# Reordered first loads, small vector steps moved to GpSimd and paired last folds in a spectral filter and token MLP kernel

## The chip, the cores and the metric

The kernel runs on one core of a Trainium2 chip. The metric is the device time of one execution in microseconds: the median of three runs is 124.67 us (124.54 to 124.88). All times below are microseconds unless a row says ns.

## The reference

Two branches work on the same x of 2048 tokens by 512 channels (bf16), and a sigmoid gate mixes them:

```python
def _A_ref(x, w_r, w_i):                       # spectral filter
    X = rfft2(x.astype(float32), axes=(-2, -1))
    X = X * (w_r + 1j * w_i)
    return irfft2(X, s=(S, D)).astype(bfloat16)

def _B_ref(x, w1, b1, w2, b2):                 # MLP over tokens
    h = _layernorm(x, axis=-1)
    u = gelu(einsum("bsd,sf->bdf", h, w1) + b1)
    y = einsum("bdf,fs->bds", u, w2) + b2
    return y.transpose(0, 2, 1)

g = sigmoid((x * gate_w).sum(-1, keepdims=True))
out = g * a + (1 - g) * b                      # a, b: the two branches; S=2048, D=512, F=1792
```

## The kernel before

The 2048 tokens lie on 128 partitions in 16 blocks of 512 channels. Block j = 4q + r holds the tokens of quarter q whose number leaves r when divided by 4.

**The MLP branch** fills most of TensorE. m1 (L710) multiplies w1 by the normalized x (h) into 14 hidden tiles; a gelu on ScalarE (L730) writes them to gl. m2 (L1103) multiplies w2 by gl into one PSUM bank y per output block, 14 matmuls each. ScalarE evicts y with the gate and the bias (yev, L1121), for the last two blocks VectorE does (fin, L1151).

**The spectral branch** takes four stages, each a set of small matmuls on TensorE, an eviction on ScalarE and sums and differences on VectorE:
- forward along the tokens: folds of x over q (q4a L550, q4s L555, q4b L560), matmuls fa (L572 to L575), copies (L578), butterflies (L584, radix4 L603 to L619);
- forward along the channels: matmuls fb (L669), copies (L673), folds eo into B (L683 to L688);
- the filter: butterfly bfly (L810), products with W (L818), comb (L823), ob (L847 to L849) back into B. Some bins need a path of their own. c0a (L786) copies the first bins of B to c0; c0b (L831 to L841) multiplies them with the filter's ends into ce; c0c (L853) puts ce back into B. nyq (L801 to L804) multiplies a single line on one partition into nn. ScalarE's queue then moves that line and eight lines of B into s9 by two DMAs ("lines"), one matmul (linem, L866) and a copy to s8 follow, and a DMA puts it back into B;
- inverse along the tokens: radix4 again, matmuls i1, i1h and i1o (L899, L913, L952 to L955), copies, folds zh, zg and zf (L926 to L971), the closing fold fq (L977, L978) once for each half h;
- inverse along the channels: matmuls i3 (L1036, L1037), evictions with the gate (L1040, L1089, L1091), a GpSimd copy "ends" (L1108), the folds L1111 to L1116, and the sum with y (L1139).

The gate: x times gate_w on VectorE (L738), row sums on ScalarE (L743), a tanh (L746), and omg (L750 to L753), four small operations that make 1 - g and the scaled bias.

**The order of the work.** Each step is added to a plan with an engine, a duration, its reads and writes and a priority. The plan runs a list schedule with these durations, in which each engine takes the ready step of the lowest priority, and the program is written out in the order that results. So each engine's queue is fixed before the run, and a queue whose next instruction waits holds back all that stands behind it.

**GpSimd's queue before.** It issues some loads, then 16 gathers of rows of the filter (L771) paced by one-element copies that wait for h or gl (L760), then the loads of the tables tg and ti, and at the end the copies L1108.

**The first loads before.** SP issues x block 0, then w1 blocks 0, 2 and 1, the table ta and w1 block 3; ScalarE issues x blocks 2, 1 and 3 before its first table load. Of the four blocks with r = 0, VectorE makes the layernorm statistics of blocks 0 and 4, ScalarE those of 8 and 12 (ASTAT).

Of the kernel before, what the change touches and what calls it, by code (L numbers as in the profile page):

```python
# [16 lines left out]
P = 128  # L17
S = 2048
D = 512
# [115 lines left out]
class Plan:  # L135
# [32 lines left out]
    def order(self):  # L168
# [17 lines left out]
        while events:  # L186
# [16 lines left out]
            while progress:  # L203
                progress = False
                for eng, ts in pending.items():
# [15 lines left out]
                    if best.pk:  # L221
                        n, size = best.pk[:2]
                        k = best.pk[2] if len(best.pk) > 2 else 16
                        work = n * (0.009 + size / 27200.0)
                        issue = max(now, lanes[-8] if len(lanes) > 7 and eng != "POOL" else 0.0) + best.dur
                        dma_free = max(dma_free, issue + 0.8) + work / 16 * (1.45 if issue < 2.0 else 1.2 if issue < 6.0 else 1.0)
# [44 lines left out]
def kernel(  # L271
# [14 lines left out]
    V, A, T = nc.vector, nc.scalar, nc.tensor  # L286
# [78 lines left out]
    add("ACT", 0.4, presq, reads=["eps"], writes=["omg"], prio=-8.85)  # L365
# [107 lines left out]
    ASTAT = (8, 12, 5, 2)  # L473
# [3 lines left out]
    for r in range(4):  # L477
# [10 lines left out]
        for n, j in enumerate(OWN[r]):  # L488
# [11 lines left out]
            else:  # L500
                add("DVE", 0.82, lambda j=j: stat(j), reads=[("x", r, j // 4)], writes=[("mv", j)], prio=pj, after=[n0] if j == 4 else ())
# [4 lines left out]
            if j == 0:  # L506
                s0 = sj
            if j == 8:
                aq.deps.add(s0)
# [9 lines left out]
            if j == 8:  # L519
                n8 = nj  # L520
# [26 lines left out]
        def q4a(r=r):  # L547
            xf = t["xf", r] = t["gl"][:, 6 + 4 * (r % 2):10 + 4 * (r % 2), :]
            xs = t["x"][:, :, r, :]
            V.tensor_sub(xf[:, 2:4], xs[:, 0:2], xs[:, 2:4])  # L550

        def q4s(r=r):
            xs = t["x"][:, :, r, :]
            s = t["st"][:, 0:1024].rearrange("p (m d) -> p m d", m=2)
            V.tensor_add(s, xs[:, 0:2], xs[:, 2:4])  # L555
# [7 lines left out]
        add("DVE", tt(1024), q4s, reads=xk, writes=["st"], prio=pq, after=[n8])  # L563
        add("DVE", tt(1024), q4a, reads=xk, writes=[("xf", r % 2)], prio=pq, alloc=["xf"])
        add("DVE", 2 * tt(512), q4b, reads=["st"], writes=[("xf", r % 2)], prio=pq)
# [157 lines left out]
    for n, (ft, j, cs) in enumerate(order):  # L723
        last = j == jorder[-1]
        bank = "fb" if 4 <= ft < NF else "acc"
        m1t.append(add("PE", mm(cs.stop - cs.start), lambda ft=ft, j=j, cs=cs: m1(ft, j, cs),
# [22 lines left out]
    def omg():  # L749
        V.tensor_scalar(t["omg"][:], t["g"][:], -0.5, 0.5, op0=Alu.mult, op1=Alu.add)  # L750
        V.tensor_scalar(t["g"][:], t["g"][:], 0.5, 0.5, op0=Alu.mult, op1=Alu.add)
        V.tensor_scalar_mul(t["g"][64:P, 1::2], t["g"][64:P, 1::2], 0.5 ** 0.5)
        V.tensor_mul(t["ombb2"][:], t["omg"][:], t["b2f"][:])  # L753
    add("DVE", 0.5, omg, reads=["b2f"], writes=["g", "omg"], prio=0)
# [29 lines left out]
    def c0a():  # L784
        b = t["B"][:, :, :, :, 0]
        V.tensor_copy(t["c0"][:, 0], b[:, :, :, 0:2])  # L786
        V.tensor_copy(t["c0"][:, 1], b[:, :, :, 3:1:-1])
    add("DVE", 0.2, c0a, reads=[("B", lt, e) for lt in range(2) for e in range(4)], writes=["c0"], prio=0.3)

    for lt in range(2):  # L790
# [3 lines left out]
        if lt == 0:  # L794
            def nyq():
# [4 lines left out]
                for i in range(2):  # L800
                    V.tensor_mul(na[:, i], v, wn[:, i, None, 0:L].to_broadcast([1, 2, L]))  # L801
                V.tensor_sub(nn[:, 0], na[:, 0, 1], na[:, 1, 0])
                V.tensor_add(nn[:, 1], na[:, 1, 1], na[:, 0, 0])
                V.tensor_mul(nn[:, ::-1, 0], t["c0"][0:1, 1, 0, 0, :], wn[:, 0, 0:257:256])  # L804
            add("DVE", 2 * tt(512) + 2 * tt(256) + 0.1, nyq, reads=bk + [("wn", 0), ("wn", 1), "c0"] + pbk, writes=["nn"], prio=0.5)
# [20 lines left out]
        if lt == 0:  # L826
            def wprep():
# [3 lines left out]
                V.tensor_add(pv[0], ends[0][:, :, 0], ends[0][:, :, 1])  # L831
                V.tensor_sub(pv[1], ends[1][:, :, 0], ends[1][:, :, 1])

            def c0b():
                wprep()
                c0, cm, ce, pm = t["c0"], t["cm"], t["ce"], t["wpm"]
                for i in range(2):
                    V.tensor_mul(cm[:, i], c0[:, i, None].rearrange("p o a e k -> p o (a e) k").to_broadcast([P, 2, 8, 2]),
                                 (pm[:] if i == 0 else pm[:, ::-1]).rearrange("p i a e k -> p i (a e) k"))
                V.tensor_sub(ce[:, 0], cm[:, 0, 0], cm[:, 1, 0])  # L840
                V.tensor_add(ce[:, 1], cm[:, 0, 1], cm[:, 1, 1])  # L841
            add("DVE", tiny(4) + 0.25, c0b, after=[cb], reads=["c0"] + [("W", c, l) for c in range(2) for l in range(2)], writes=["ce"], prio=0.3)
# [73 lines left out]
    for h in range(2):  # L916
# [13 lines left out]
        def zg(h=h):  # L930
            e, o = t["zp"][:, h, 0], t["zp"][:, h, 1]
            z = t["zz"][:, h, 1].rearrange("p v k r a -> p r (v k) a")[:, 1::2]
            V.tensor_add(z[:, :, :, 0:64], e, o)
            V.tensor_sub(e, e, o)
            V.tensor_sub(z[:, :, 0::2, 64:P], e[:, :, 0::2], e[:, :, 1::2])
            V.tensor_add(z[:, :, 1::2, 64:P], e[:, :, 0::2], e[:, :, 1::2])
        add("DVE", 2 * tt(512) + 2 * tt(256), zg, reads=[("zp", h, 0), ("zp", h, 1)], writes=[("zz", h, 1, 1), ("zz", h, 3, 1)], prio=3.55)

        for r in (0, 2):
# [21 lines left out]
            def zf(h=h, r=r):  # L961
                e = t["ze"][:, h, r // 2]
                k0, k1 = (t["zz"][:, h, :, :, k, r, :] for k in range(2))
                if r == 0:
                    V.tensor_copy(k0[:, :, :, 0], e[:, :, :, 0])
                    V.tensor_copy(k1[:, :, :, 0], e[:, :, :, P])
# [5 lines left out]
            add("DVE", 2 * tt(512) + (tiny(2) if r == 0 else 0), zf, reads=[("ze", h, r, lt) for lt in range(2)], writes=[("zz", h, r, lt) for lt in range(2)], prio=3.55)  # L972
# [6 lines left out]
        add("DVE", 2 * tt(2048), fq, reads=[("zz", h, r, lt) for r in range(4) for lt in range(2)] + [("T", 0, 0), ("T", 0, 1), ("T", 1, 0), ("T", 1, 1)], writes=["xs" if h == 0 else "pp", ("z", h)], prio=3.54 if h == 0 else 3.6)  # L979
# [93 lines left out]
    for grp in groups:  # L1073
        for j in grp:
# [35 lines left out]
            def fold(e, o, s):  # L1110
                V.tensor_add(s[:, 0, :, 1:P], e[:, :, 1:P], e[:, :, P + 1:L])  # L1111
                V.tensor_sub(s[:, 1, :, P - 1:0:-1], e[:, :, 1:P], e[:, :, P + 1:L])
                sv = s.rearrange("p k (j h) d -> p j h k d", h=2)
                for u in range(o.shape[1]) if o.shape[1] == 1 else (slice(None),):
                    V.tensor_add(o[:, u, 0:4:3], sv[:, u, 0], sv[:, u, 1])
                    V.tensor_sub(o[:, u, 2:0:-1], sv[:, u, 0], sv[:, u, 1])  # L1116
            quart = lambda v: v.rearrange("p j h (k d) -> p j (h k) d", k=2)

            if j < LATE:
# [4 lines left out]
                if j % 2 == 0:  # L1124
                    continue

                def pair(j=j):
                    return (epair(j // 2 % NEO) if j > 1 else t["e0"]).rearrange("p j h d -> p (j h) d")
                ek = [("eo", 0, 0), ("eo", 0, 1)] if j == 1 else [("eo", j - 1), ("eo", j)]
                add("POOL", 0.4, lambda j=j, ends=ends, pair=pair: ends(pair(), espair(j // 2)), reads=ek, writes=[("es", j // 2 % 2)], prio=4)  # L1130

                def es(j=j, fold=fold, quart=quart, pair=pair):
                    fold(pair(), quart(epair(NEO + j // 2 % NOB)), espair(j // 2))
                add("DVE", 4 * tt(512), es, reads=ek + [("es", j // 2 % 2)], writes=[("ob", j)], prio=4, alloc=["ob"], free=["eo"] if j > 1 else ())

                def fin(j=j):
                    tbuf(j)
                    o = t["tb_"][:, j - 1:j + 1]
                    V.tensor_add(o, o, epair(NEO + j // 2 % NOB))  # L1139
                add("DVE", tt(1024), fin, reads=[("ob", j)], writes=[("o", j - 1), ("o", j)], prio=4, free=["ob"])  # L1140
            else:
                add("POOL", 0.4, lambda j=j, ends=ends: ends(epair(j // 2 % NEO)[:, j % 2], espair(j)[:, :, 0:2]), reads=[("eo", j)], writes=[("es", j % 2)], prio=4)

                def es(j=j, fold=fold, quart=quart):
                    fold(epair(j // 2 % NEO)[:, j % 2], quart(tbuf(j)[:, None]), espair(j)[:, :, 0:2])
                add("DVE", 4 * tt(256), es, reads=[("eo", j), ("es", j % 2)], writes=[("o", j)], prio=4, free=["eo"] if j % 2 else (), after=gates)

                for n, cs in enumerate(parts):
                    def fin(j=j, n=n, cs=cs):
                        o = tbuf(j).rearrange("p h d -> p (h d)")[:, cs]  # L1150
                        V.scalar_tensor_tensor(o, t["y", j, n][:, cs], t["omg"][:, j:j + 1], o, op0=Alu.mult, op1=Alu.add)  # L1151
                    add("DVE", d1(cs.stop - cs.start) + 0.1, fin, reads=[("y", j, n), "omg", ("o", j)], writes=[("of", j, n)], prio=1,
                        free=[("acc", "fa")[n]])

# [41 lines left out]
```

## Time and profile before

| | before |
|---|---|
| median of three runs | 124.67 us |
| profiled execution, its own time | 124.94 us |
| its span in the trace | 123.2 us |
| TensorE's first m1 matmul, end of the last m2 | 5.06, 120.34 us |
| TensorE, VectorE, ScalarE, GpSimd busy | 118.0, 113.8, 84.9, 42.2 us |
| granted TensorE clock | 1.0 |

Times in the rows count from the start of the span. A row of the timeline gives the start, the busy time, the engine (DVE is VectorE, ACT ScalarE, POOL GpSimd, SP the sync engine's DMA queue), the line, the operation and its tiles and shapes. In brackets stands how long the engine was idle before, and what ended that. A row of the chain in order of time gives the start, the length and the step.

### The profile page before, as it was taken

To read this page: it belongs to the slowest core of one execution; us is meant where nothing else is said; L and a number is where in the kernel's file an instruction comes from. 1 tells how busy PE (TensorE), PEld (TensorE's weight loads), DVE (VectorE), ACT (ScalarE), POOL (GpSimd) and SP (SyncE) were. 2 spreads that over 40 slices of the span, in tenths; PEclk is the share of its full clock that TensorE was granted. 3 is DMA by queue.
4 is the path that set the end of the run, shared out by engine and by line. 5 is a ranking of instruction groups with operands and counts; after the bars stand their busy time and mean duration, and the time that the engine had idled before them with its cause. 6 is when DMAs were issued, how large, how long until landed. Compare 5 with 4: busy or idle time off the path is not lost.

```text
span 123.2 us, 2197 instructions
## 1 busy us (share of the span) xinstructions
PE 118.0 (96%) x760; PEld 65.6 (53%) x774; DVE 113.8 (92%) x248; ACT 84.9 (69%) x182; POOL 42.2 (34%) x57
## 2 busy tenths in 40 slices
PE   6998999999999999999999999999999999999990
PEld 2454555546544666444455545557565566655570
DVE  1799999999999979999999999999999999999991
ACT  3869999997998699988420047238993369979500
POOL 6502428988089984889100000000000002112300
PEclk9999999999999999999999999999999999999999
DMA  3999999999999999999728800000000000214062
GB/s 95 286 366 365 366 374 195 245 351 324 340 289 197 169 284 385 397 406 343 222 39 318 340 0 3 0 0 5 3 0 5 1 0 3 118 55 176 0 255 85
DMA packets 16765, 22.80 MB, mean 185 GB/s; under 512 B 3216, under 2 KB 13858, under 8 KB 16754
## 3 DMA queue, kind: packets, MB, share of 16 engines
q1 hardware_dynamic: 15122, 19.71, 51.7%
q0 software_dynamic: 1152, 2.55, 7.5%
q10 hardware_dynamic: 480, 0.40, 1.0%
q8 instruction: 6, 0.10, 0.4%
q14 instruction: 5, 0.04, 0.1%
HBM read 20.54 MB, written 2.10 MB: 184 GB/s over the span
## 4 chain that ended last, share of the span: by engine, by line
PE 87%; DMA 7%; ACT 2%; issue 1%; DVE 0%; SPq 0%
PE acc L1103 39%; PE acc L710 30%; DMA x<-in_A_x_dram 7%; PE fb L710 4%; PE fb L669 1%; PE fa L669 1%; PE fa L574 1%; PE fa L575 1%; PE fa L572 1%; PE fa L1036 1%; PE fa L913 1%; PE fb L1037 1%; PE fa L1037 1%; PE fb L1036 1%; PE fa L899 1%
## 5 line engine op out<-in xcount | busy, mean ns | idle before, releaser
L1103 PE MATMUL acc<-gl,wb 128*128 128x512 bf16 (+1 forms) x124 | 31.3, 376 | 0.3 <-issue 0.2
L710 PE MATMUL acc<-h,wb 128*128 128x512 bf16 x124 | 29.7, 379 | 0.2
L1103 PE MATMUL acc<-gl,wa 128*128 128x512 bf16 (+1 forms) x93 | 23.5, 376 | 0.2
L1103 PEld LDWEIGHTS <-wb 128*128 128x128 bf16 x136 | 14.4, 113 | 10.6 <-issue 0.2
L710 PEld LDWEIGHTS <-wb 128*128 128x128 bf16 x128 | 12.2, 98 | 12.4
L1121 ACT ACTIVATE x<-acc,ombb,omg 128x512 bf16<-128x512 f32 x14 | 11.0, 784 | 10.0 <-PE acc L1103 7.6
L710 PE MATMUL acc<-h,wa 128*128 128x512 bf16 (+1 forms) x67 | 16.9, 371 | 0.0
L1108 POOL COPY st<-zo 128x8 bf16<-128x8 bf16 x1 | 0.4, 442 | 42.9 <-DVE zo L1061 42.9
L1103 PEld LDWEIGHTS <-wa 128*128 128x128 bf16 x102 | 10.8, 113 | 7.8
L710 PEld LDWEIGHTS <-wa 128*128 128x128 bf16 x102 | 10.0, 99 | 9.2 <-DMA wa<-in_B_w_dram 0.9
L771 POOL DMA_INDIRECT W<-in_A_w_i_dram,ix x8 | 14.1, 1766 | 1.8 <-issue 1.8
L730 ACT ACTIVATE gl<-acc,b1f 128x512 bf16<-128x512 f32 x12 | 8.3, 693 | 4.6 <-PE acc L710 4.5
L482 DVE BATCH_NORM_STATS2 stats<-x 128x6 f32<-128x512 bf16 x12 | 8.2, 680 | 2.2 <-DMA x<-in_A_x_dram 2.2
L743 ACT ACTIVATE x<-x 128x512 bf16<-128x512 bf16 x16 | 9.9, 623 | 0.0
L771 POOL DMA_INDIRECT W<-in_A_w_r_dram,ix x8 | 9.3, 1166 | 1.6 <-issue 1.3
L710 PE MATMUL fb<-h,wa 128*128 128x512 bf16 (+1 forms) x32 | 9.6, 366 | 0.1
L578 ACT CAST xp<-fa 128x512 bf16<-128x512 f32 x16 | 8.9, 578 | 1.0 <-issue 0.6
L1108 POOL COPY st<-X 128x8 bf16<-128x8 bf16 (+1 forms) x8 | 3.2, 412 | 11.7 <-ACT X L1040 8.8
L543 ACT ACTIVATE h<-x,nmr,rstd 128x512 bf16<-128x512 bf16 x8 | 6.3, 803 | 0.0
L868 ACT CAST s<-fa 8x512 bf16<-8x512 f32 x1 | 0.6, 575 | 8.2 <-PE fa L866 8.2
L669 PEld LDWEIGHTS <-X 128*128 128x128 bf16 x64 | 4.7, 98 | 2.4 <-issue 0.2
L760 POOL COPY hold<-gl 1x1 bf16<-1x1 bf16 x6 | 4.2, 695 | 4.8 <-ACT gl L730 4.8
(190 smaller groups left out, 254.2 us busy)
## 6 DMA issues: line engine op xcount, KB each, us to landing
wb<-in_B_w_dram SPq DMA_DIRECT2D x8, 512.0 KB
wb<-in_B_w_dram SPq DMA_DIRECT2D x2, 2048.0 KB
wa<-in_B_w_dram SPq DMA_DIRECT2D x1, 3072.0 KB
wa<-in_B_w_dram SPq DMA_DIRECT2D x2, 768.0 KB
out_dram<-x SPq DMA_DIRECT2D x3, 512.0 KB
x<-in_A_x_dram SPq DMA_DIRECT2D x2, 512.0 KB
wa<-in_B_w_dram SPq DMA_DIRECT2D x4, 192.0 KB
wa<-in_B_w_dram SPq DMA_DIRECT2D x2, 384.0 KB
```

What stands on the lines that cost most here:

```text
L482: V.bn_stats(out=t["stats"][:, j, :], in_=t["x"][:, j // 4, j % 4, :])
L543: add("ACT", act(512, 2), lambda j=j: A.activation(t["h"][:, j // 4, j % 4, :], t["x"][:, j // 4, j % 4, :], ActF.Identity, bias=t["nmr"][ ...
L578: add("ACT", act(512), lambda r=r, dq=dq: A.copy(xa(r)[:, :, :, dq, :], t["pa", r, dq][:]), reads=[("pa", r, dq)], writes=[("X", r % 2, dq ...
L669: T.matmul(pb[:, q, :, b, :], lhsT=t["X"][:, lt, e, c, 2 * b + q, :], rhs=t["tb"][:, k:k + 128], start=True, stop=True)
L710: T.matmul(t["u", ft][:, cs], lhsT=w[:, j // 4, j % 4, c * P:(c + 1) * P], rhs=t["h"][:, j // 4, j % 4, cs], start=(j == jorder[0] and not ...
L730: gelus.append(add("ACT", act(512, 1), lambda ft=ft: A.activation(t["gl"][:, ft, :], t["u", ft][:], ActF.Gelu_apprx_tanh, bias=t["b1f"][:, ...
L743: A.activation(t["x"][:, q, r, :], t["x"][:, q, r, :], ActF.Copy, accum_out=t["glog"][:, 4 * q + r:4 * q + r + 1])
L760: nc.gpsimd.tensor_copy(t["hold"][:], t["h"][0:1, n // 4, n % 4, 511:512] if kind == "h" else t["gl"][0:1, n, 0:1])
L771: add("POOL", 1.15, lambda comp=comp, lt=lt, e=e: nc.gpsimd.indirect_dma_start(out=t["W"][:, comp, lt, e, 1, 0:257], out_offset=None, in_= ...
L1103: T.matmul(t["y", j, n][:, cs], lhsT=w[:, o, 512 * q + r:512 * q + 512:4], rhs=t["gl"][:, ft, cs], start=(ft == 0), stop=(ft == NFT - 1))
L1108: nc.gpsimd.tensor_copy(s[:, :, :, 0], e[:, :, 0:129:128].rearrange("p m k -> p k m"))
L1121: A.activation(tbuf(j).rearrange("p h d -> p (h d)"), t["y", j, 0][:], ActF.Identity, bias=t["ombb2"][:, j:j + 1], scale=t["omg"][:, j:j + 1])
```

## The change

It has three parts. The line numbers of the steps in the changed kernel are higher by 2 to 20.

First, SP issues x block 0, x block 2, w1 block 0, x block 1, and w1 blocks 2, 1 and 3; ScalarE loads its table first and then issues x block 3 and ta. Statistics of block 8 go to VectorE and those of block 4 to ScalarE. The folds q4a and q4s of r = 0 are split in two halves, the first of them before the first h. Some durations and priorities of the plan change with it.

Second, omg, c0a, nyq, c0b and the two small copies of zf (now zc) are issued on GpSimd instead of VectorE.

Third, the fold of the last stage is split into two steps, folda and foldb, and blocks 14 and 15 are folded as one pair, as the others are, with their y added after. zg is split into zga and zgb, with its difference written to st instead of in place.

```diff
-    ld_x0(2, "ACT", -9)
+    ld_x0(2, "SP", -8.95)
     ld_w10(0, "SP", -8.9)
-    ld_x0(1, "ACT", -8.9)
-    ld_x0(3, "ACT", -8.88)
+    ld_x0(1, "SP", -8.85)
+    ld_x0(3, "ACT", -8.9)
...
-    ld_ta(0, -8.65)
+    ld_ta(0, -8.8, "ACT")
...
-    add("ACT", 0.4, presq, reads=["eps"], writes=["omg"], prio=-8.85)
+    add("ACT", 1.6, presq, reads=["eps"], writes=["omg"], prio=-8.95)
...
-    ASTAT = (8, 12, 5, 2)
+    ASTAT = (4, 12, 5)
...
+        if r == 0:
+            for m in range(2):
+                xm = [("x", 0, m), ("x", 0, m + 2)]
+                add("DVE", tt(512), lambda q4a=q4a, m=m: q4a(m=slice(m, m + 1)), reads=xm, writes=[("xf", 0, m)], prio=pq,
+                    alloc=[] if m else ["xf"], after=[n8] if m else ())
+                add("DVE", tt(512), lambda q4s=q4s, m=m: q4s(m=slice(m, m + 1)), reads=xm, writes=[("st", m)], prio=pq,
+                    after=[n8] if m else [b8])
...
     def omg():
-        V.tensor_scalar(t["omg"][:], t["g"][:], -0.5, 0.5, op0=Alu.mult, op1=Alu.add)
+        G.tensor_scalar(t["omg"][:], t["g"][:], -0.5, 0.5, op0=Alu.mult, op1=Alu.add)
...
-    add("DVE", 0.5, omg, reads=["b2f"], writes=["g", "omg"], prio=0)
+    add("POOL", 1.2, omg, reads=["b2f"], writes=["g", "omg"], prio=0)
...
-        V.tensor_copy(t["c0"][:, 0], b[:, :, :, 0:2])
-        V.tensor_copy(t["c0"][:, 1], b[:, :, :, 3:1:-1])
-    add("DVE", 0.2, c0a, reads=[("B", lt, e) for lt in range(2) for e in range(4)], writes=["c0"], prio=0.3)
+        G.tensor_copy(t["c0"][:, 0], b[:, :, :, 0:2])
+        G.tensor_copy(t["c0"][:, 1], b[:, :, :, 3:1:-1])
+    add("POOL", 0.7, c0a, reads=[("B", lt, e) for lt in range(2) for e in range(4)], writes=["c0"], prio=0.3)
...
                 for i in range(2):
-                    V.tensor_mul(na[:, i], v, wn[:, i, None, 0:L].to_broadcast([1, 2, L]))
+                    G.tensor_mul(na[:, i], v, wn[:, i, None, 0:L].to_broadcast([1, 2, L]))
...
-            add("DVE", 2 * tt(512) + 2 * tt(256) + 0.1, nyq, reads=bk + [("wn", 0), ("wn", 1), "c0"] + pbk, writes=["nn"], prio=0.5)
+            add("POOL", 3.2, nyq, reads=bk + [("wn", 0), ("wn", 1), "c0"] + pbk, writes=["nn"], prio=0.5)
...
-                V.tensor_add(pv[0], ends[0][:, :, 0], ends[0][:, :, 1])
-                V.tensor_sub(pv[1], ends[1][:, :, 0], ends[1][:, :, 1])
+                G.tensor_add(pv[0], ends[0][:, :, 0], ends[0][:, :, 1])
+                G.tensor_sub(pv[1], ends[1][:, :, 0], ends[1][:, :, 1])
...
-            add("DVE", tiny(4) + 0.25, c0b, after=[cb], reads=["c0"] + [("W", c, l) for c in range(2) for l in range(2)], writes=["ce"], prio=0.3)
+            add("POOL", 2.0, c0b, reads=["c0"] + [("W", c, l) for c in range(2) for l in range(2)], writes=["ce"], prio=0.3)
...
+            if r == 0:
+                def zc(h=h):
+                    e = t["ze"][:, h, 0]
+                    G.tensor_copy(t["zz"][:, h, :, :, 0, 0, 0], e[:, :, :, 0])
+                    G.tensor_copy(t["zz"][:, h, :, :, 1, 0, 0], e[:, :, :, P])
+                add("POOL", 0.7, zc, reads=[("ze", h, 0, lt) for lt in range(2)], writes=[("zc", h)], prio=3.5)
...
+            if j % 2:
+                k = j // 2
...
+                add("DVE", 2 * tt(512), lambda k=k, pair=pair, folda=folda: folda(pair(), espair(k)), reads=ek, writes=[("ef", k % 2)], prio=4,
+                    free=["eo"] if j > 1 else ())
+                add("DVE", 2 * tt(512), lambda k=k, obuf=obuf, foldb=foldb: foldb(obuf(), espair(k)), reads=[("es", k % 2), ("ef", k % 2)],
+                    writes=ok, prio=4, alloc=["ob"] if j < LATE else (), after=gates)
```

More of the change, by code (lines that the diff above doesn't have):

```diff
@@ L500 @@
             else:
-                add("DVE", 0.82, lambda j=j: stat(j), reads=[("x", r, j // 4)], writes=[("mv", j)], prio=pj, after=[n0] if j == 4 else ())
+                bj = add("DVE", 0.82, lambda j=j: stat(j), reads=[("x", r, j // 4)], writes=[("mv", j)], prio=pj, after=[n0] if j == 8 else ())
             sj = add("ACT", 0.28, lambda j=j: sq(t["rstd"][:, j:j + 1], t["mv"][:, j, 1:2], 1.0 / D if j in ASTAT else 1.0),
@@ L562 @@
         pq = -1.65 if r == 0 else 1.2 * r + 1.2 + QS
-        add("DVE", tt(1024), q4s, reads=xk, writes=["st"], prio=pq, after=[n8])
-        add("DVE", tt(1024), q4a, reads=xk, writes=[("xf", r % 2)], prio=pq, alloc=["xf"])
-        add("DVE", 2 * tt(512), q4b, reads=["st"], writes=[("xf", r % 2)], prio=pq)
+        if r == 0:
[5 more added lines that the diff above has]
+                    after=[n8] if m else [b8])
+        else:
+            add("DVE", tt(1024), q4s, reads=xk, writes=["st"], prio=pq)
+            add("DVE", tt(1024), q4a, reads=xk, writes=[("xf", r % 2)], prio=pq, alloc=["xf"])
+        add("DVE", 2 * tt(512), q4b, reads=["st"] + ([(k, *e, m) for k, e in (("st", ()), ("xf", (0,))) for m in range(2)] if r == 0 else []), writes=[("xf", r % 2)], prio=pq)
         for dq in range(4):
@@ L971, in zf @@
                     V.tensor_sub(k1[:, :, :, ::-1], e[:, :, :, 0:P], e[:, :, :, P:L])
-            add("DVE", 2 * tt(512) + (tiny(2) if r == 0 else 0), zf, reads=[("ze", h, r, lt) for lt in range(2)], writes=[("zz", h, r, lt) for lt in range(2)], prio=3.55)
+            add("DVE", 2 * tt(512), zf, reads=[("ze", h, r, lt) for lt in range(2)], writes=[("zz", h, r, lt) for lt in range(2)], prio=3.55)
+            if r == 0:
[4 more added lines that the diff above has]
+                add("POOL", 0.7, zc, reads=[("ze", h, 0, lt) for lt in range(2)], writes=[("zc", h)], prio=3.5)
         def fq(h=h):
@@ L1129 @@
                 ek = [("eo", 0, 0), ("eo", 0, 1)] if j == 1 else [("eo", j - 1), ("eo", j)]
[L1130 to L1134, printed above, removed]
@@ L1136, in fin @@
-                def fin(j=j):
-                    tbuf(j)
[L1138 to L1153, printed above, removed]
@@ new lines, with obuf @@
+                ok = [("ob", j)] if j < LATE else [("o", j - 1), ("o", j)]
+                def obuf(j=j):
+                    tbuf(j)
+                    return epair(NEO + j // 2 % NOB) if j < LATE else t["tb_"][:, j - 1:j + 1]
+                add("POOL", 0.4, lambda k=k, ends=ends, pair=pair: ends(pair(), espair(k)), reads=ek, writes=[("es", k % 2)], prio=4)
+                add("DVE", 2 * tt(512), lambda k=k, pair=pair, folda=folda: folda(pair(), espair(k)), reads=ek, writes=[("ef", k % 2)], prio=4,
+                    free=["eo"] if j > 1 else ())
@@ new lines, with fin @@
+                add("DVE", 2 * tt(512), lambda k=k, obuf=obuf, foldb=foldb: foldb(obuf(), espair(k)), reads=[("es", k % 2), ("ef", k % 2)],
+                    writes=ok, prio=4, alloc=["ob"] if j < LATE else (), after=gates)
+                if j < LATE:
+                    def fin(j=j, obuf=obuf):
+                        o = t["tb_"][:, j - 1:j + 1]
+                        V.tensor_add(o, o, obuf())
+                    add("DVE", tt(1024), fin, reads=[("ob", j)], writes=[("o", j - 1), ("o", j)], prio=4, free=["ob"])
@@ new lines, with fin @@
+    for j in range(LATE, NJ):
+        for n, cs in enumerate([slice(0, D)] if j < NJ - 1 else [slice(0, 384), slice(384, D)]):
+            def fin(j=j, n=n, cs=cs):
+                o = tbuf(j).rearrange("p h d -> p (h d)")[:, cs]
+                V.scalar_tensor_tensor(o, t["y", j, n][:, cs], t["omg"][:, j:j + 1], o, op0=Alu.mult, op1=Alu.add)
+            add("DVE", d1(cs.stop - cs.start) + 0.1, fin, reads=[("y", j, n), "omg", ("o", j)], writes=[("of", j, n)], prio=1,
+                free=[("acc", "fa")[n]])
@@ L1155 @@
+    for grp in groups:
+        parts = [slice(0, D)] if grp[-1] < NJ - 1 else [slice(0, 384), slice(384, D)]
         for n, cs in enumerate(parts):
```

76 lines of the change are left out of this document (38 added, 38 removed).

## The prediction

> **What bounds the kernel now.** I read the page first, parts 1 and 4.
>
> ```profile
> PE 118.0 (96%) x760; PEld 65.6 (53%) x774; DVE 113.8 (92%) x248; ACT 84.9 (69%) x182; POOL 42.2 (34%) x57
> PE 87%; DMA 7%; ACT 2%; issue 1%; DVE 0%; SPq 0%
> ```
>
> TensorE is busy 96% and holds 87% of the chain, but VectorE is at 92%: work taken off VectorE pays only where TensorE has a wait to lose. The timeline and the chain in order of time, read together, tell where TensorE is not dense:
>
> ```profile
> 9.25 0.73 ACT gl L492 x2
> 10.00 0.81 ACT gl L496 x2
> ...
> 11.18 0.48 ACT xp L578
> 11.71 0.22 PE fa L572
> ...
> 100.44 0.06 PE fa L1036
> ...
> 120.38 0.35 DVE x L1151
> ```
>
> TensorE's first real matmul starts at 5.06 (timeline), the last ends at 120.34. Between, starts follow each other at 0.2155 us for a 512-column matmul, except before 11.71, where L572 waited 0.58 for ScalarE's L578 copies. Some 0.6 us is all that TensorE can gain inside, plus what it starts earlier; the nine warm-up matmuls end at 4.82, so that is at most 0.24.
>
> Then VectorE's timeline, because four of its steps move to GpSimd:
>
> ```profile
> 54.29 0.17 DVE L786 CAST c<-B 128x16 f32<-128x16 bf16 x1
> ...
> 56.76 0.74 DVE L801 TENSOR_TENSOR X<-B,wn 1x512 bf16<-1x512 bf16 x2
> ...
> 63.50 0.18 DVE L831 TENSOR_TENSOR wpm<-W 128x16 f32<-128x16 bf16 x1
> ...
> 66.77 0.21 DVE L853 CAST B<-ce 128x16 bf16<-128x16 f32 x1
> ...
> 98.86 1.22 DVE L978 TENSOR_TENSOR xp<-X 128x2048 bf16<-128x2048 bf16 x1
> ```
>
> From 49 to 119 this queue stands nowhere for more than 0.2 us. L853 is the step to watch: it consumes ce, and everything of the inverse transform stands behind it on VectorE. Last, GpSimd's timeline, for the time at which it could take new work:
>
> ```profile
> 49.64 1.00 POOL L760 COPY hold<-gl 1x1 bf16<-1x1 bf16 x1 [1.61 <-ACT gl L730]
> ...
> 54.67 3.00 POOL L771 DMA_INDIRECT W<-in_A_w_i_dram,ix  x1 [0.30 <-issue]
> 57.66 0.61 POOL L312 DMA_DIRECT2D tg<-dft_tg  x1
> 58.22 0.63 POOL L312 DMA_DIRECT2D rot<-dft_ti  x1
> ```
>
> GpSimd is not free before 58.85, while B, the input of c0a, is complete at 54.3.
>
> **The loads and the first tiles.** SP now issues x block 0, x block 2, w1 block 0, x block 1; ScalarE loads its table first (1.28, the ACT_TABLE_LOAD row) and issues x block 3 about 0.7 later. In the trace of before w1 block 0 releases TensorE at 5.00 and h's first half is ready at the same time (L513, two halves of 0.3 from 4.66), so both would have to come earlier. VectorE gets a 512-element subtraction (0.42 in the rows of that shape) between the first statistics and h, where it stood 0.36 for rstd. Bounds for TensorE's start: 0.24 earlier, 0.1 later. The built order has two more m1 matmuls (0.43) ahead of the L572 that waited, while ScalarE's sums and its L578 copies stand as before, so of 0.58 about 0.15 remains. I take 0.45 earlier for all of this.
>
> **The GpSimd chain.** In the built order c0a, nyq, c0b and omg stand in that order behind the last gather, tg and ti. Ahead of nyq's first multiply the program holds one instruction more than the source: a reload of GpSimd's code library, which before has none of. Step by step:
> - Free: the wait at 49.64 ends with a gelu and moves with TensorE, 58.85 - 0.45 = 58.4.
> - c0a, two copies of 128x16. Nearest row: L1108's GpSimd copies of 128x8, about 0.4. Two: 0.8. VectorE's price is the lower end, 0.26 from 54.29 to 54.55.
> - The reload. No row shows one. From below: 0, if it costs nothing, or the 1.28 of ACT_TABLE_LOAD. From above: the page's instruction packets,
>
> ```profile
> q8 instruction: 6, 0.10, 0.4%
> ```
>
>   which are 0.4% of 16 x 123.2, 7.9 us, 1.3 for each 16 KB packet. A library is code that must come over such a path, not a table of an engine, so I stand near the upper row: five packets one after the other, 6.6. The Trainium skill (GPSIMD Engine Reference, Instruction dispatch) says that the first call to a freshly loaded kernel pays about 6 us, with no instruction for it in the profile; by 5.95 the result below would be 131.0. No run so far shows it.
> - nyq, five two-input operations on one partition. Lower end: VectorE's 1.44 (56.76 to 58.20). Upper end: five times 1.14, the longest L760 copy of one element (40.63). No GpSimd row has two inputs; I take L760's mean of 0.695, as the nearest of a GpSimd operation beside a busy VectorE: 3.5.
> - c0b, six operations of 128x16 and 128x32. Lower end 0.90 (63.50 to 64.40), upper end 6 x 1.14 = 6.8; I take 0.41 as for c0a, since VectorE will be standing: 2.5.
>
> ce is ready at 58.4 + 0.8 + 6.6 + 3.5 + 2.5 = 71.8.
>
> **Who waits.** VectorE's queue loses c0a (0.26), nyq (1.57 to the next start), omg (0.69) and c0b (0.81), 3.33 in all, and would reach c0c's L853 at 66.77 - 3.33 = 63.4. It is in order, so it stands there until 71.8: 8.4 us of new wait for 3.3 of work saved. (Part of it may come earlier, at ob, which overwrites the B that nyq reads; the end is the same.) Behind it stand both rounds of the inverse transform and all folds. On ScalarE's queue the two line DMAs wait for nn and B, and every later eviction stands behind them; on TensorE's, the line matmul stands in order after 40 m2 matmuls, as before. omg is last in GpSimd's chain, four times 0.41 later, at 73.4; it hides behind the line matmul, since the evictions that need it come after that.
>
> Two routes to TensorE's end:
> - By the line matmul and i1. Before, the line matmul came at 71.90, 4.9 after L853's end; now 72.0 + 4.9 = 76.9, where TensorE would arrive at 71.5. That is the first stall. The first i1 started at 82.48, 0.29 after its input; the input moves by 71.8 - 66.8 = 5.0, so i1 starts at 87.5. From there TensorE needed 120.34 - 82.48 = 37.86; the new order has 9 m2 more behind i1 (78 ahead instead of 87), 9 x 0.2155 = 1.94. End: 127.3.
> - By the last fold of the inverse. From L853 to the end of L978 (100.08) is 33.3; the zc copies leave it (0.15 + 0.14). z is ready at 71.8 + 33.0 = 104.8; the first i3 came 0.36 later, then 19.90 to the end, and 10 m2 more behind it, 2.15. End: 127.2.
>
> They agree: 127.3 + 2.86 (the tail from 120.34 to 123.2: last L1151, last store) = 130.2 span. The profiled execution's own time was 124.94, 1.74 above its span, and 0.27 above the median of 124.67. So 130.2 + 1.74 - 0.27 = 131.6.
>
> **Edits with no effect on the end.** The zc copies on GpSimd (0.7 a pair at the row's 0.35 each) run beside the zf folds and are needed by fq some 2 to 4 us later; without that cover they cost that 0.7 each. The split of zg keeps its four operations. Rows 14 and 15 folded as a pair take four operations of 0.42 instead of eight of 0.29, 117.02 to 119.03: some 0.6 off VectorE. But its folds would end at 119.03 + 5.0 - 0.3 - 0.6 = 123.1, well before TensorE's last output at 127, so nothing comes of it. One GpSimd copy for both rows replaces two; it hides in the same slack.
>
> **Rivals.**
> - *The chain is late, but the reload is small.* With 1.28, ce is at 66.5 and everything ends 5.3 earlier: 126.3. For it: the two engine table loads in this trace take just that. Against: they load a table, and a library is code.
> - *Faster.* No time for the reload, and small operations at about VectorE's price. The stall disappears when ce comes by about 64.2; then TensorE ends at 120.34 - 0.6 = 119.7, and the time is 124.0. The two kernels are equal at ce = 127.3 - 120.34 = 7.0 before 71.8, 64.8: 6.4 us for the whole GpSimd chain from 58.4. My own operations without a reload already take 6.8, so this needs both a free reload and cheaper operations. VectorE's prices (2.6) say that it is possible.
> - *GpSimd's operations are stretched throughout*, nyq and c0b at 1.14 each: 12.5 instead of 6.0, giving 138. For it: the same one-element copy takes from 0.18 to 1.14 in this trace, and a gather from 0.97 to 3.00. Against: VectorE is idle for most of this time. The Trainium skill (SBUF, two separate sides) says that GpSimd and a two-input VectorE operation hold one port pair exclusively; by that rule the operations after 63.4 run unhindered, which speaks against this rival.
>
> **Numbers.** Forecast 0.70; small reload 0.11; faster 0.09; stretched 0.10. The likeliest gives 131.6. Low end: 126.0, just below the small reload. High end: the reload at 7.9 and half of the stretch, 131.6 + 1.3 + 3.3, some 136.5. Outside it stand the faster case and the far end of the stretched one. A difference of 0.3% is 0.37 us, about what a measurement can tell. Faster 0.09; same 0.03, a chain that lands by chance near 64.8; slower 0.88.
>
> **What would show it.** In the changed trace: GpSimd idle for some 6 us between its second c0 copy and nyq's first multiply; VectorE idle at ob or L863 until GpSimd's last ce operation, 6 to 10 us in all; TensorE standing once before the line matmul and again before the first i1; the folds' last step well before the last matmul. I am wrong if the reload leaves no gap, if ce lands before 64, or if VectorE does not stand before L863.

## The result and the profile after

The changed kernel takes 131.51 us (median of 6 runs, 129.14 to 131.76), against 124.78 for the kernel before in the same runs (124.54 to 125.12). The ratio is 1.039, with an interval of 1.033 to 1.046. It is taken from the two shortest runs, 129.14 and 130.31, since runs more than 1.5% above the shortest are left out of it; the medians alone give 1.054. The profiled execution took 131.36, with a span of 129.5. The forecast of 131.6 lies on the median, and 1.9 above the 129.7 that the ratio of 1.039 gives. The number came out, but not the way it was made up.

Parts 1 and 4 of the page of the changed kernel, and the row of the granted clock from part 2:

```profile
PEclk9999999999999999999999999958999999999999
...
PE 121.6 (94%) x774; PEld 66.8 (52%) x774; DVE 114.1 (88%) x227; ACT 82.9 (64%) x178; POOL 58.9 (45%) x77
...
PE 54%; POOL 21%; DVE 9%; issue 8%; DMA 4%; ACT 2%; SPq 1%; POOLq 0%; DVEq 0%
```

GpSimd held nothing of the chain before and now holds 21% of it. VectorE has 21 instructions fewer (227 against 248) and is busy 0.3 us longer. The first says that GpSimd now stands in the way; the second suggests that it slows VectorE down as well, which the rows of VectorE below bear out. The timeline of GpSimd shows the moved steps:

```profile
60.73 0.61 POOL L312 DMA_DIRECT2D rot<-dft_ti  x1
61.29 0.32 POOL L796 CAST c<-B 128x16 f32<-128x16 bf16 x1
61.57 0.19 POOL L797 CAST c<-B 128x16 f32<-128x16 bf16 x1
61.83 4.01 POOL L811 TENSOR_TENSOR X<-B,wn 1x512 bf16<-1x512 bf16 x2
65.92 1.53 POOL L812 TENSOR_TENSOR X<-X 1x256 bf16<-1x256 bf16 x1
...
70.31 0.22 POOL L851 TENSOR_TENSOR ce<-cm 128x16 f32<-128x16 f32 x1
```

GpSimd comes free at 61.34, c0a ends at 61.76, and 0.07 later nyq's first multiply starts: the reload leaves no gap. nyq lasts to 69.13, and ce is ready at 70.53. VectorE's timeline beside it:

```profile
61.59 1.26 DVE L833 TENSOR_TENSOR xp<-xp,st 128x2048 bf16<-128x2048 bf16 x1
62.78 2.17 DVE L834 TENSOR_TENSOR xp<-st,xp 128x2048 bf16<-128x2048 bf16 x1
65.05 1.88 DVE L857 TENSOR_TENSOR B<-xp 128x2048 bf16<-128x2048 bf16 x1
66.85 1.15 DVE L858 TENSOR_TENSOR B<-xp 128x1024 bf16<-128x1024 bf16 x1
67.92 1.15 DVE L859 TENSOR_TENSOR B<-xp 128x1024 bf16<-128x1024 bf16 x1
70.56 0.21 DVE L863 CAST B<-ce 128x16 bf16<-128x16 f32 x1 [1.49 <-POOL ce L851]
```

In the kernel before these shapes take 1.22 and 0.68:

```profile
62.36 1.22 DVE L824 TENSOR_TENSOR xp<-st,xp 128x2048 bf16<-128x2048 bf16 x1
...
65.45 0.68 DVE L848 TENSOR_TENSOR B<-xp 128x1024 bf16<-128x1024 bf16 x1
```

Only 1.49 of the loss is a plain wait for ce; some 2.6 hides in operations (L834 to L859) that look merely long. TensorE's timeline at the two places where it stands, and the window with the clock (columns: length; busy time and count of PE, PEld, DVE, ACT, POOL; granted clock; DMA share; GB/s):

```profile
6.36 1.03 PE L720 MATMUL acc<-h,wa 128*128 128x256 bf16 x4 [1.34 <-DMA wa<-in_B_w_dram]
...
85.49 0.29 PE L968 MATMUL fa<-rot,B 128*128 128x129 bf16 x1 [2.79 <-DVE B L618]
```

```profile
84.00:88.20 4.20, 2.71 (x17) 1.85 (x18) 4.20 (x7) 1.07 (x2) 0.00 (x0) 0.59 0.00 0
```

In the kernel before, the first i1 follows an m2 without a wait:

```profile
82.31 0.22 PE L952 MATMUL fa<-rot,B 128*128 128x129 bf16 x1
```

TensorE's last matmul ends at 126.74, 6.40 later than before (120.34), and the time of the profiled execution is 6.42 longer. The 6.40 is 3.18 by which the first i1 starts later (85.49 against 82.31), 9 x 0.2155 = 1.94 of m2 that now stand behind i1, and the remaining 1.28. That remainder fits the clock, which has a mean of 0.59 in this window: the trace records it at 0.5 from 84.74 to 88.16, and TensorE, which works again from 85.49, loses half of these 2.67 us, 1.3. The fall of the clock belongs to this execution and does not set the time alone: among the six, those with a granted clock of 1.0 or 0.999 took 129.14, 131.67 and 131.69.

### The profile page after: what moved, and what is told of

Same layout as the page of the kernel before. It is cut to its first block, busy times and chain, and to the rows that moved or that the text cites. A ratio compares the mean times of both kernels' runs of the same rounds, so it can differ in the third digit from the quotient of the medians.

```text
span 129.5 us, 2223 instructions
## 1 busy us (share of the span) xinstructions
PE 121.6 (94%) x774; PEld 66.8 (52%) x774; DVE 114.1 (88%) x227; ACT 82.9 (64%) x178; POOL 58.9 (45%) x77
## 4 chain that ended last, share of the span: by engine, by line
PE 54%; POOL 21%; DVE 9%; issue 8%; DMA 4%; ACT 2%; SPq 1%; POOLq 0%; DVEq 0%
PE acc L1123 24%; PE acc L720 12%; POOL W L781 10%; PE fb L720 6%; DMA wa<-in_B_w_dram 4%; POOL X L811 3%; POOL hold L770 3%; DVE st L828 2%; PE fa L585 1%; PE fa L584 1%; POOL X L812 1%; DVE B L857 1%; DVE xp L833 1%; DVE xp L821 1%; ACT gl L740 1%
## 5 line engine op out<-in xcount | busy, mean ns | idle before, releaser
L1123 PE MATMUL acc<-gl,wb 128*128 128x512 bf16 (+1 forms) x128 | 33.5, 382 | 0.0
L720 PE MATMUL acc<-h,wb 128*128 128x512 bf16 x128 | 30.2, 379 | 0.0
L720 PE MATMUL acc<-h,wa 128*128 128x512 bf16 (+1 forms) x68 | 18.2, 390 | 1.3 <-DMA wa<-in_B_w_dram 1.3
L720 PEld LDWEIGHTS <-wa 128*128 128x128 bf16 x102 | 10.6, 105 | 12.0 <-DMA wa<-in_B_w_dram 2.2
L1123 PEld LDWEIGHTS <-wa 128*128 128x128 bf16 x102 | 11.0, 113 | 8.1
L482 DVE BATCH_NORM_STATS2 stats<-x 128x6 f32<-128x512 bf16 x13 | 8.8, 680 | 2.0 <-DMA x<-in_A_x_dram 2.0
L990 POOL COPY X<-wt 128x4 bf16<-128x4 bf16 x2 | 1.0, 490 | 21.0 <-ACT wt L974 21.0
L720 PE MATMUL fb<-h,wa 128*128 128x512 bf16 (+1 forms) x34 | 10.4, 384 | 0.0
L1128 POOL COPY st<-X 128x8 bf16<-128x8 bf16 x7 | 3.9, 557 | 11.3 <-ACT X L1060 6.8
L486 ACT ACTIVATE rstd<-mv,eps 128x1 f32<-128x1 f32 x16 | 4.6, 293 | 3.7 <-DVE mv L483 2.5
L974 ACT CAST wt<-fa 128x512 bf16<-128x512 f32 x4 | 2.3, 598 | 5.7 <-PE fa L971 5.7
```

The lines of the kernel that those rows point to most:

```text
L482: V.bn_stats(out=t["stats"][:, j, :], in_=t["x"][:, j // 4, j % 4, :])
L486: A.activation(o, v, ActF.Abs_reciprocal_sqrt, bias=t["eps"][:, 0:1], scale=scale)
L720: T.matmul(t["u", ft][:, cs], lhsT=w[:, j // 4, j % 4, c * P:(c + 1) * P], rhs=t["h"][:, j // 4, j % 4, cs], start=(j == jorder[0] and not ...
L1123: T.matmul(t["y", j, n][:, cs], lhsT=w[:, o, 512 * q + r:512 * q + 512:4], rhs=t["gl"][:, ft, cs], start=(ft == 0), stop=(ft == NFT - 1))
L1128: nc.gpsimd.tensor_copy(s[:, :, :, 0], e[:, :, 0:129:128].rearrange("p m k -> p k m"))
```

## The experiments

In every table and text of this section, times inside a run are from its profiled execution. "before" is run again beside each group: 125.07, 124.92 and 124.87.

**The chain alone.** Parts 2 and 3 of the change with the old loads (no_loads).

```diff
     ld_x0(0, "SP", -9)
-    ld_x0(2, "SP", -8.95)
+    ld_x0(2, "ACT", -9)
...
-    ASTAT = (4, 12, 5)
+    ASTAT = (8, 12, 5, 2)
```

> The kernel before with the second and third part (small steps on GpSimd, paired folds), with the first loads as before. Theory A: GpSimd is free at 58.85 instead of 61.3, its chain to ce takes the 9.2 us of the changed kernel, ce is ready at 68.1, TensorE ends 56.2 later at 124.3, and the time is about 128.6. Theory B: all of the loss is the chain, so about 131.5, as the whole change.

Measured: 131.58, ratio 1.054 (1.049 to 1.059), the time of the second theory. All of the loss is here without the new loads. The first theory missed: GpSimd came free at 60.83 and not at 58.85, ce is ready at 69.76 and not at 68.1, and TensorE ends 57.05 behind it and not 56.2. The plan also puts omg ahead of c0b here.

**The loads alone** (loads_only: the kernel before with part 1, the reverse of the diff above), and **more warm-up matmuls** in the whole change, so that TensorE's clock would not be withheld after the late first tile:

> The kernel before with the first part alone (the order of the first loads, block 8's statistics on VectorE, the split first folds). Theory A, two delays: the change's first m1 matmul came at 6.36 instead of 5.06 because w1 block 0 landed at 6.31, and TensorE then ran at half its speed until 9.65; that is some 2.9 us by then, less the 0.58 wait that is gone, so this kernel alone should take about 127.0 us. Theory B, the GpSimd chain alone, as predicted: the new loads gain 0.45, so 124.2.

```diff
-    NWARM = 9
+    NWARM = 13
```

> The whole change with 13 warm-up matmuls instead of 9, so that TensorE is busy until its first m1 matmul. Theory A: TensorE runs at full speed from about 5.5 on, and the 1.6 us lost to half speed between 6.36 and 9.65 are won back; GpSimd's chain starts as much earlier: 129.9. If the late landing alone matters and not the speed: 131.5.

Measured: loads_only 126.23, ratio 1.012 (1.004 to 1.020); warm13 131.67, 1.052 (1.044 to 1.059). So the new loads cost 1.2 by themselves: TensorE waits 1.7 for w1's first block and starts m1 at 6.42 instead of 5.06. In the whole change they add nothing to the medians; I take it that TensorE would only have stood longer at i1, which no run shows by itself. With 13 warm-ups the full clock is on record from 4.21 on, and nothing was gained. This test is not clean: the plan came out differently with it (73 m2 ahead of i1 for 78, omg ahead of c0b, ce at 72.05), and loads_only has the full clock from 4.29 with nine warm-ups.

**Where the first load's loss is.** The load order alone, with the first ta at its old place on SP's queue:

```diff
-    ld_ta(0, -8.8, "ACT")
+    ld_ta(0, -8.65)
```

> The kernel before with the new load order alone, but the first ta load at its old place on SP's queue. Theory A (the early ta and the fourth x block on ScalarE's queue share the engines with w1's first block and delay it by 1.3 us): without ta in front, w1's first block lands near 5.6 instead of 6.3, the first m1 matmul near 5.7, and half of the 1.2 us of the load order alone comes back: 125.3 to 125.8 against 126.2. Theory B (x's blocks ahead of w1 in one queue delay it, whatever ta does): w1 lands near 6.2 as before and the time stays at 126.0 to 126.4.

Measured: 127.44, ratio 1.020 (1.013 to 1.027). The first m1 came at 5.60, as the first theory has it, but the time did not follow; it is longer than with ta on ScalarE's queue. VectorE now stands 0.55 and 0.75 near 9 and 11 us for later blocks of x, and TensorE for h. Both theories missed: what arrives earlier in one place is missing in another. Which of the transfers sets the price stays open.

**nyq back on VectorE**, all else of the change kept:

```diff
-                    G.tensor_mul(na[:, i], v, wn[:, i, None, 0:L].to_broadcast([1, 2, L]))
+                    V.tensor_mul(na[:, i], v, wn[:, i, None, 0:L].to_broadcast([1, 2, L]))
...
-            add("POOL", 3.2, nyq, ...
+            add("DVE", 2 * tt(512) + 2 * tt(256) + 0.1, nyq, ...
```

> The whole change, but with nyq's five operations on VectorE as before. Theory A: ce is ready at about 61.3 + 0.5 + 1.4 = 63.2, VectorE doesn't stand, and only the late start is left: about 127.0. Theory B: without the chain the change is worth what the prediction's faster case says, 124.0 to 124.2. If instead the other GpSimd operations hold VectorE up as well, 129 or more.

Measured: 126.61, ratio 1.011 (1.006 to 1.016), what the loads cost alone. By the medians nyq's place decides 4.9 of the 6.7; by the ratios, 1.039 and 1.011, it is 3.5 of 4.9. The order that the plan then chooses is part of it (84 m2 ahead of i1 for 78). But the rest is not free, and ce came at 68.30, not at the 63.2 of the first theory: c0b's two 128x32 multiplies, 0.23 each where VectorE stands, took 3.44 here beside a busy VectorE.

**nyq alone on GpSimd** (the kernel before, with only nyq's five operations moved):

```diff
-                    V.tensor_mul(na[:, i], v, wn[:, i, None, 0:L].to_broadcast([1, 2, L]))
+                    G.tensor_mul(na[:, i], v, wn[:, i, None, 0:L].to_broadcast([1, 2, L]))
...
```

> The kernel before with one edit: the five two-input operations of nyq run on GpSimd; c0a, c0b, omg and all loads and folds stay as before. Theory A (the loss is a queue: c0b and omg stand behind nyq on GpSimd, and VectorE stands for ce): with c0b back on VectorE nothing on VectorE waits for the end of nyq except the writers over its inputs, the two multiplies start near 59 and even at 2.0 us each are done at 63, before ob at 64.3; the time stays near before's 125.0 (124.4 to 125.5). Theory B (GpSimd operations cost VectorE their own length again, wherever c0b is): nyq is about 7 us long beside L818, L823, L824 and ob, those lose about 3 us in all, VectorE saves 1.4 by giving nyq away, c0c moves from 66.8 to about 68.4 and the time to 126.3 to 127.

Measured: 127.59, ratio 1.022 (1.016 to 1.027). No step of VectorE waits for the end of nyq here, and it is slower all the same; the queue theory falls as the whole cause. VectorE's timeline:

```profile
56.45 3.24 DVE L818 TENSOR_TENSOR st<-xp,W 128x4096 bf16<-128x4096 bf16 x1
59.72 1.95 DVE L823 TENSOR_TENSOR xp<-xp,st 128x2048 bf16<-128x2048 bf16 x1
61.59 1.68 DVE L824 TENSOR_TENSOR xp<-st,xp 128x2048 bf16<-128x2048 bf16 x1
```

Against 2.29, 1.22 and 1.22 before, these three lose 2.1, and VectorE had given away 1.44; GpSimd needs 8.2 for nyq (55.87 to 64.10). The time is above the 126.3 to 127 of the second theory as well: TensorE stands 1.7 at i1, behind 82 m2 for 87 (the table below).

**What stretches.** Three pairs of multiplies that nothing uses, in the shape of nyq's first two, on GpSimd in the kernel before (probe):

```diff
+    def probe():
+        s9, d = t["s9"], t["B"][0:1, 0, 0, 0:2, 0:256]
+        for i in range(2):
+            nc.gpsimd.tensor_mul(d, s9[0:1, 0:512].rearrange("p (v l) -> p v l", v=2),
+                                 s9[0:1, None, 0:256].to_broadcast([1, 2, 256]))
...
```

> The kernel before with six more GpSimd multiplies that nothing uses (1x512 bf16 from zeros, the shape of nyq's first two), in three pairs: one pair at about 1 us, while VectorE has nothing to do; one near 11 us, beside VectorE's statistics and tile copies; one near 31 us, beside VectorE's 2048-element products. Theory A (nyq is long because GpSimd and VectorE stretch each other): the first pair takes 1.0 to 1.3 us an operation, the third pair about 2 us, and the VectorE operations beside it take up to twice their time before (L738 about 1.18 each). Theory B (2 us is GpSimd's own time for this operation): all three pairs take about 2 us each and VectorE beside them keeps its times. If a load of the GpSimd code library costs about 6 us, the DMA issues after the first pair, or the pair itself, show such a gap; if it costs nothing, none does.

Measured, the timelines of GpSimd and of VectorE:

```profile
1.31 2.24 POOL L349 TENSOR_TENSOR B<-s 1x512 bf16<-1x512 bf16 x2 [0.86 <-DVE s L326]
...
10.95 2.25 POOL L349 TENSOR_TENSOR B<-s 1x512 bf16<-1x512 bf16 x2
...
29.26 3.86 POOL L349 TENSOR_TENSOR B<-s 1x512 bf16<-1x512 bf16 x2
```

```profile
10.94 2.41 DVE L521 TENSOR_SCALAR h<-x,mv,rstd 128x512 bf16<-128x512 bf16 x2
...
28.92 3.25 DVE L746 TENSOR_TENSOR x<-x,gw 128x2048 bf16<-128x2048 bf16 x2
32.10 1.58 DVE L592 TENSOR_TENSOR X<-xp 128x1024 bf16<-128x1024 bf16 x1
```

Beside an idle VectorE the pair takes 2.24, 1.12 each; that is the operation's own length. The third pair takes 1.93 each. Near 11 us GpSimd kept its length, and VectorE's pair took 2.41 instead of the 0.74 of the same two operations before. Near 31 us both lost: 3.86 for 2.24, and VectorE 3.25 for 2.35 and 1.58 for 0.69. No gap of some 6 us stands before the first pair: GpSimd is idle for 0.86, until VectorE's memset ends at 1.22, and the pair starts 0.09 later. The run took 127.72 in its one timing, 2.8 us more than the kernel before, for six unused operations on an engine off the critical path. The plan moved a little too (85 m2 ahead of i1 for 87).

**The small operations without nyq** (small_pool: c0a, c0b, omg and zc on GpSimd, nyq on VectorE, old loads, folds in two steps; the change without its first part and without the nyq edit). Against the kernel before, its core is:

```diff
-        V.tensor_copy(t["c0"][:, 0], b[:, :, :, 0:2])
+        G.tensor_copy(t["c0"][:, 0], b[:, :, :, 0:2])
...
-                V.tensor_sub(ce[:, 0], cm[:, 0, 0], cm[:, 1, 0])
+                G.tensor_sub(ce[:, 0], cm[:, 0, 0], cm[:, 1, 0])
```

> The whole change without nyq on GpSimd and without the new load order: c0a, c0b, omg and the zc copies on GpSimd, the folds in two steps, nyq on VectorE. Theory A (only nyq ahead of c0b makes ce late): ce is ready near 65 to 67 about when VectorE reaches c0c, TensorE goes on as in the kernel before: 124.3 to 125.5. Theory B (any two-input operation on GpSimd beside a busy VectorE is stretched, c0b too: 1.1 to 2.2 us each as in the run with nyq back on VectorE, where ce came at 68.3): c0c 2 us later than before, 126 to 127.

Measured: 126.77, ratio 1.016 (1.010 to 1.022), with ce at 67.07. The first theory is wrong in the time. The second has the time, but not the way: c0c came 0.34 later than before (67.11 for 66.77), not 2. TensorE reached its first i1 earlier and stood 1.3 for it, since the planner had put it behind 81 m2 instead of 87.

**TensorE's order.** The planner took the moved work for a gain and moved i1 forward. Two runs put it back by one planned duration, with no instruction added or removed; in chain_late_i1 it is no_loads with

```diff
-        add("DVE", 0.15, c0c, reads=["ce"], writes=bk, prio=pr)
+        add("DVE", 0.15 if lt == 0 else 2.5, c0c, reads=["ce"], writes=bk, prio=pr)
```

and in small_late_i1 small_pool with 1.0 in place of 2.5.

> Parts 2 and 3 of the change on the old loads (131.6 in its own run), with one number of the planner changed: c0c of the second half is planned at 2.5 instead of 0.15, so that the first i1 matmul stands behind 87 m2 matmuls on TensorE, as in the kernel before, and not behind 76; the line matmul stays behind 40, and no instruction is added or removed. Theory A (part of the loss is TensorE's order: the planner put i1 11 m2 forward, because it held VectorE for relieved, and TensorE stands for i1 while m2 that could run stand behind it): 11 m2 of 0.376 fill the 3.6 us before i1, TensorE's end goes from 126.8 to about 123.3 and the time to 127.6 to 128.5. Theory B (VectorE's later arrival is the bound by itself, so that work moved ahead of i1 is missing behind it): TensorE stands that long later, before the last transforms, and the time stays at 130.5 to 131.6.

> c0a, c0b, omg and zc on GpSimd with nyq on VectorE, old loads, folds in two steps (126.8 in its own run), with c0c of the second half planned at 1.0 instead of 0.15, which puts the first i1 matmul behind 85 m2 instead of 81. Theory A (the stall of 1.5 us at i1 is all that this version loses): 125.1 to 125.5, within 0.5% of the kernel before and perhaps below it. Theory B (VectorE's 0.3 us later c0c and the turns that GpSimd's zc copies take beside VectorE cost the rest): 126.0 to 126.8.

Measured: 127.64, ratio 1.021 (1.018 to 1.025), and 125.48, ratio 1.005 (1.003 to 1.007). The first theory holds in both; the wait lists of TensorE for no_loads, and then for chain_late_i1, say it directly (waiter, releaser: us in total, times, longest):

```profile
PE fa L958 <- DVE B L608: 3.2, 1, 3.2
```

```profile
PE fa L958 <- DVE B L608: 0.8, 1, 0.8
```

| | nyq | ce ready | m2 ahead of i1 | wait at i1 | TensorE's end | median |
|---|---|---|---|---|---|---|
| before | VectorE | 64.40 | 87 | none | 120.34 | 124.78 |
| whole change | GpSimd | 70.53 | 78 | 2.8 | 126.74 | 131.51 |
| no_loads | GpSimd | 69.76 | 76 | 3.2 | 126.81 | 131.58 |
| chain_late_i1 | GpSimd | 70.13 | 87 | 0.8 | 123.52 | 127.64 |
| nyq_only | GpSimd | 65.46 | 82 | 1.7 | 122.69 | 127.59 |
| small_pool | VectorE | 67.07 | 81 | 1.3 | 121.82 | 126.77 |
| small_late_i1 | VectorE | 66.86 | 85 | 0.2 | 120.47 | 125.48 |

From no_loads to chain_late_i1 the chain on GpSimd is as late, and 3.7 of its 6.5 us are gone, each against its own kernel before (6.51 and 2.77). (I had priced an m2 at its duration of 0.376; matmuls start 0.2155 apart, so the 11 m2 fill 2.4. The rest, some 1.3 between the first i1 and TensorE's end, goes with the clock, which was at 0.5 from 85.71 to 89.12 in no_loads, just after the wait, and stayed at 1.0 in chain_late_i1.)

In small_late_i1 the timeline also shows how the two engines share (GpSimd and VectorE rows):

```profile
58.80 0.20 POOL L750 TENSOR_SCALAR omg<-g 128x16 f32<-128x16 f32 x1 [0.30 <-ACT g L746]
59.08 2.12 POOL L751 TENSOR_SCALAR g<-g 128x16 f32<-128x16 f32 x1
61.28 1.22 POOL L752 TENSOR_SCALAR g<-g 64x8 f32<-64x8 f32 x1
...
58.81 2.32 DVE L818 TENSOR_TENSOR st<-xp,W 128x4096 bf16<-128x4096 bf16 x1
61.17 1.23 DVE L823 TENSOR_TENSOR xp<-xp,st 128x2048 bf16<-128x2048 bf16 x1
62.31 1.22 DVE L824 TENSOR_TENSOR xp<-st,xp 128x2048 bf16<-128x2048 bf16 x1
```

The same 128x16 operation takes 0.20 when it gets in ahead of L818, and 2.12 when it comes after it has begun: it ends at 61.20, just after L818 (61.13). The next ends at 62.50, just after L823 (62.40). In these rows GpSimd waits until the VectorE operation has ended.

**The folds** (part 3 alone on the kernel before):

```diff
-            def fold(e, o, s):
+            def folda(e, s):
...
+            def foldb(o, s):
```

> The kernel before with part 3 alone: zg in two steps, rows 14 and 15 folded as a pair in two steps, nothing new on GpSimd but one ends copy fewer. Theory A (hidden: VectorE's folds end before TensorE's last matmul in the kernel before as well): no difference, 124.7 to 125.1. Theory B (VectorE's 0.6 us less work at the end brings the last store forward): 124.3 to 124.6.

Measured: 124.87 against 124.87, ratio 1.000 (0.998 to 1.002). No effect, by the first theory. No version tried beats the kernel before.

## Why the prediction was right in its number and half wrong in its reason

**Held.** ce, late on GpSimd, sets the end. ce came at 70.53 for a predicted 71.8, the first i1 at 85.49 for 87.5, TensorE's end at 126.74 for 127.3. The 9 m2 behind i1 are there (78 ahead instead of 87). TensorE stood before i1, VectorE before L863, and the last fold ended at 122.2 (predicted 123.1), ahead of the last matmul. Part 3 has no effect (folds_only). c0a took 0.42 for 0.8, c0b 1.4 for 2.5; both small.

**Did not show.** VectorE's wait before L863 was 1.49, where 8.4 had been forecast; the rest of its delay came earlier and inside its operations. TensorE's first stall, before the line matmul, did not come at all: the line matmul ran at 74.00 (forecast 76.9) without a wait.

**Fell: the reload, 6.6.** This was the first of the signs named for being wrong, and it came: between c0a and nyq lie 0.07 at 61.76. I had raised a price from the instruction packets of part 3 of the page that no row tied to this step; queue q8 has 6 packets in the kernel before and 6 in the changed one. The Trainium skill (GPSIMD Engine Reference, Instruction dispatch) gives about 6 us for the first call of a freshly loaded kernel; no run here shows it, and the 0.07 speaks against it for this step.

**Mis-sized: nyq, 3.5.** It took 7.3. The step took its price from one-element copies. The five operations have an own length (1.12 for a 512 multiply) and, on top of it, the turns that they wait for. This error hangs on the first: with the reload, the sum had nyq start at 65.8, when VectorE would stand; without it, nyq ran from 61.83 beside a VectorE that was still busy.

**Wrong: the free time of GpSimd, 58.4.** It was 61.34. The loads were to bring 0.45 and instead put TensorE's first m1 1.30 later, at 6.36: ScalarE's queue issued x block 3 at 1.00 and ta at 1.44, beside its table load and not behind it, and w1's block 0 landed at 6.31 instead of 4.96. With the loads alone (loads_only) GpSimd comes free at 60.59, 1.74 later than before; what makes the other 0.75 is not shown. With the old loads GpSimd is late by another way: in no_loads it comes free at 60.83, because the last gather takes longer.

```profile
54.71 4.94 POOL L771 DMA_INDIRECT W<-in_A_w_i_dram,ix  x1 [0.30 <-issue]
```

The gather waits for VectorE, too. In the kernel before it takes 3.00 and ends 0.81 after VectorE's first L818 (56.85), behind which nyq stood; in no_loads, where nyq is gone from VectorE, it ends 0.82 after the second L818 (58.83). In nyq_only it starts ahead of L818 and takes 0.94. Why it gets no turn between the two in no_loads is open.

So the sum held because errors cancelled: -6.5 for the reload, +3.8 for nyq, +2.9 for the free time, -0.4 and -1.1 for c0a and c0b, -1.3 in all at ce. Behind ce the sum lacked the fall of the clock (+1.3) and put i1 15.7 behind ce, where 15.0 were measured: in the kernel before the first i1 did not follow its input at once, since L608 ends at 81.59 and TensorE was at m2 until 82.31. That the total met the median is luck. (One slip of the working changes nothing: the high end adds up to 136.2, not 136.5.)

**The rival that was dismissed too soon** is the stretched one. It was held at 0.10 by the remark that VectorE would be idle from 63.4. VectorE came to L863 only at 69.07, 5.7 later: 2.8 because it was late already (L698, its last fold into B, ends at 57.18, for 54.39 before; it had stood 1.28 and 1.04 for rstd in the first 20 us, and has one more block's statistics), and 2.6 more because GpSimd stretched it. VectorE was busy beside nyq almost from its start to its end (69.07 and 69.13). The Trainium skill (SBUF — State Buffer, SBUF: two separate sides) says that the engine that starts first holds the shared ports for its whole instruction and the other fully blocks. The trace agrees, 0.20 against 2.12 in small_late_i1. I had applied the rule to a time at which it did not yet apply.

**TensorE's order** entered as 1.94 and was worth more. The planner believed VectorE relieved, put i1 forward, and so bought a wait and, behind the wait, a clock at half speed: 3.7 of the loss in no_loads (chain_late_i1).

## What to carry to other kernels

Work that goes from a full engine to an idle one must be priced at both ends: here a GpSimd operation of 1.12 beside VectorE's two-input operations cost each of them the other's turn, so that 1.44 us of VectorE's work became 7.3 on GpSimd and 2.1 to 2.6 lost on VectorE. When a planner's durations are wrong for the moved work, it also reorders the other engines for a gain that does not come; check how many independent matmuls stand ahead of the first dependent one. And two errors that cancel give a good number: judge a forecast by the gaps that it named, not by its total.

## What the runs showed of the hardware beyond expectation

- GpSimd and VectorE took turns by whole operations, with no row of it as idle time: the wait is inside the busy time of the operation (2.12 for 0.20). It is not only two-input operations that wait: VectorE's pair of TENSOR_SCALAR took 2.41 for 0.74 in the probe, and GpSimd's last gather 4.94 in no_loads for 0.94 in nyq_only.
- Where TensorE waited 1.9 (warm13), 2.8 (whole change) and 3.2 us (no_loads) at i1, its granted clock fell to 0.5 for 3.41 us, from inside the wait (84.74 in the whole change) or from 1.0 to 1.1 after its end (no_loads, warm13). After waits of 1.7 (nyq_only) and 0.8 (chain_late_i1) it did not.
- In the changed kernel's profiled execution the full clock is on record only from 9.65, and until then m1's first matmuls of 256 columns came 0.21 apart. In loads_only, with the same loads and nine warm-ups too, it is on record from 4.29, and the same matmuls came 0.11 apart.
- DMA issues on ScalarE's queue ran at 1.00 and 1.44, inside that engine's table load (0.74 to 2.02):

```profile
0.74 1.28 ACT L364 ACT_TABLE_LOAD   x1 [0.74 <-PEq L1200]
1.00 0.40 ACTq L312 DMA_DIRECT2D x<-in_A_x_dram  x1
```
